# Reordering work around the matrix engine: block order, result order, half exponentials and one chunk's attention

**Chip, cores, metric.** One Trainium2 chip, one core. The time is the device time of one execution in microseconds, as a median of several executions. TensorE is called PE, VectorE DVE, ScalarE ACT, GpSimd POOL, as in the profile.

## The reference, cut to what matters

```python
# q, k, v: (8 batches, 8 heads, 576 positions, 64). Heads 0-3: local mask, heads 4-7: strided mask.
scores = np.where(masks, q @ k.T / 8, -1e9)
attn   = exp(scores - max); attn /= attn.sum()
x = (attn @ v) as (4608 tokens, 512)
h = x @ w_in                                   # 512 -> 2048        "layer 1"
g = np.maximum(h, 0) + alpha * np.minimum(h, 0)
out = g @ w_out                                # 2048 -> 512        "layer 2"
```

## The kernel before

The 4608 tokens are nine chunks of 512, numbered from 0. While PE works through the two layers of chunk n, pieces of the attention of a later batch are put between its matmuls: a score group S (into `sp` and two buffers `sph`), an attention product (PV, into `pv`), a transpose (`xp`). The kernel fixes the order on each engine. PSUM, which takes what PE computes, holds three banks for layers (`hb`), two for `sp`, and three small buffers (tag `ps`) that `sph`, `pv`, `xp` take in turn. From chunk 2 on, layer 2 works with sums and differences of blocks of g (`gsum`) and of the weights (`wsum`), so that seven products of half size do for eight.

```python
def score_both(P):                      # S: half of the scores in sp, half in two sph buffers
    ...
            if i == 0:
                nc.scalar.activation(<et from sp>, Exp); nc.gpsimd.tensor_tensor(<mask>)
                continue
            def ex(y):
                nc.scalar.activation(<half y of et from sph[y]>, Exp)
                if y: nc.gpsimd.tensor_tensor(<mask>)
            defer.extend([lambda: ex(0), lambda: ex(1)])       # one is taken per step

def pv_piece(P, a):                     # PV and its normalization
    ... nc.tensor.matmul(pv, et, v16) ...
    nc.vector.reciprocal(rc, pv[sums]); nc.vector.tensor_tensor(P.x16, pv, rc, mult)

def attn_step(end):                     # one step of attention between two pieces of a layer
    if pos["i"] < end: pieces[pos["i"]][1](); pos["i"] += 1
    while late:  late.pop(0)()          # layer-1 result gT of the block just computed
    if defer:    defer.pop(0)()

def lin1_piece(n, m):                   # layer 1, block m: 4 matmuls of 512 columns into hbank()
    ... nc.tensor.matmul(hps, win16, xT) x 4
    nc.scalar.activation(neg, hps, Relu, scale=-1)
    late.append(<nc.vector.scalar_tensor_tensor(gT[m], neg, 1-alpha, hps)>)   # frees the bank

for n in range(1, 9):
    for i in range(30):                 # (32 for n = 1)
        if i < 16: lin1_piece(n, 8 * (i % 2) + i // 2)   # for n > 1: 0, 8, 1, 9, ... 14, 7, 15
        else:
            lin2_sums(n, i - 16)        # i = 16: the DVE sums begin
            if n == 2 and i == 20: w_sums(nc.vector, (3,))
        acc += left / (19 if n == 6 else 20.5) * (0.5 if i < 16 else 1.0)
        ...                             # int(acc) attention steps follow
```

The softmax here doesn't subtract the row's maximum and nothing guards it: scores larger than these inputs give would overflow.

Of the kernel before, what the change touches and what calls it, by code (L numbers as in the profile page):

```python
# [31 lines left out]
def kernel(  # L32
# [13 lines left out]
    B, H, S, D = q.shape  # L46
# [37 lines left out]
    def hbank():  # L84

        z = next(z for z in turn if z not in busy)
        turn.remove(z)
        turn.append(z)
        return banks[z]
# [243 lines left out]
    def run_masks(P=None):  # L333

        for z in list(dmask):
            z[0] += P is None
            if z[0] > 1 or z[1] is P:
                z[2]()
                dmask.remove(z)
# [55 lines left out]
        keep(nc.gpsimd.tensor_tensor(ev, ev, m, op=ALU.mult))  # L395

    defer, defer_et = [], {}

    def score_both(P):

        w, r = P.w, 72 if P.strided else 128
        for i in range(2):
            et = ets[ectr["i"] % NE]
            ectr["i"] += 1
            if i:
                sps = [pspool.tile([128, 512], F32, tag="ps", name="sph") for _ in range(2)]
            else:
                sp = pbpool.tile([128, 2, 512], F32, tag="sp", name="sp")
                sps = [sp[:, y] for y in range(2)]
            grp = P.sgroups[i]  # L410
            n = w * len(grp)
            for x, t in enumerate(grp):
                if P.dx:
                    q0 = k0 = 80 * (4 * (2 * P.pr + t % 2) + t // 2)
                else:
                    q0, k0 = w * t, 32 + 72 * t if P.strided else 96 * t
                for y in range(2):
                    hf = slice(64 * y, 64 * y + 64)
                    keep(nc.tensor.matmul(  # L419
                        sps[y][:, w * x : w * x + w], P.kT[hf, k0 : k0 + 128],  # L420
                        P.qT[hf, q0 : q0 + w], start=(x == 0), stop=(x == len(grp) - 1),
                        skip_group_check=True))
                    P.et[(2 * (t // 2) + y, t % 2) if P.strided else (t, y)] = (et, n * y + w * x)
            ev = et[0:r, 0 : 2 * n]
            if not P.strided and i == 0:
                mv = ev.rearrange("r (y c) -> r y c", y=2)
                m = mfirst.unsqueeze(1).to_broadcast([r, 2, n])
            else:
                mv = ev.rearrange("r (c f) -> r c f", f=w)
                m = (mstr if P.strided else mother).unsqueeze(1).to_broadcast([r, 2 * n // w, w])  # L430
            if i == 0:
                keep(nc.scalar.activation(  # L432
                    ev.rearrange("r (y c) -> r y c", y=2), sp[0:r, :, 0:n], AF.Exp, scale=SCALE))
                keep(nc.gpsimd.tensor_tensor(mv, mv, m, op=ALU.mult))  # L434
                continue

            def ex(y):
                keep(nc.scalar.activation(  # L438
                    ev[:, n * y : n * y + n], sps[y][0:r, 0:n], AF.Exp, scale=SCALE))
                if y:  # L440
                    keep(nc.gpsimd.tensor_tensor(mv, mv, m, op=ALU.mult))  # L441

            defer_et["et"] = et
            defer.extend([lambda: ex(0), lambda: ex(1)])

    def pv_piece(P, a):
        run_masks(P)
        while defer and any(P.et[z][0] is defer_et["et"] for z in P.et):
            defer.pop(0)()
        if P.x16 is None:  # L450
            if P.xd and P.strided:
                P.x16 = x16s
            else:
                P.x16 = xpool.tile([128, 1024], F16, tag="x16", name="x16")
        v16 = cast16[(P.b, P.strided, "v")]
        grp = P.pgroups[a]
        r = 72 if P.strided else 128
        pv = pspool.tile([128, 512], F32, tag="ps", name="pv")
        nb = 2 * len(grp)
        for x in range(nb):  # L460
            t, hh = grp[x // 2], x % 2
            et, c = P.et[(t, hh)]
            keep(nc.tensor.matmul(  # L463
                pv[:, 65 * x : 65 * x + 65], et[0:r, c : c + 128],
                v16[0:r, 2 * P.pr + hh, t, :] if P.strided else v16[:, 6 * (2 * P.pr + hh) + t, :],
                start=(x == 0), stop=(x == nb - 1), skip_group_check=True))
        w = P.w
        rc = rpool.tile([128, 8], F32, tag="rc", name="rc")
        pvv = pv[0:w, 0 : 65 * nb].rearrange("r (c e) -> r c e", e=65)
        keep(nc.vector.reciprocal(rc[0:w, 0:nb], pvv[:, :, 64]))  # L470
        c0 = 128 * grp[0]
        keep(nc.vector.tensor_tensor(  # L472
            P.x16[0:w, c0 : c0 + 64 * nb].rearrange("r (c e) -> r c e", e=64),
            pvv[:, :, 0:64],
            rc[0:w, 0:nb].unsqueeze(2).to_broadcast([w, nb, 64]), op=ALU.mult))
# [75 lines left out]
    for g in range(7, npair + 2):  # L551
# [30 lines left out]
        for i, (kind, fn) in enumerate(seq):  # L582
            extra = []
            if todo and i in nslots:
                left = len([z for z in nslots if z >= i])
# [31 lines left out]
    def attn_until(b):  # L617

        return max(i for i, (g, _) in enumerate(pieces) if g == 4 * b + 3) + 1

    late = []

    def attn_step(end):
        run_masks()
# [11 lines left out]
    def lin1_piece(n, m):  # L636
        if m == 0:
            gTs[n] = gpool.tile([128, 16, 512], F16, tag="gT", name="gT")
        c0 = (512 * n) % RING
        parts = [(c0, 0, min(512, RING - c0))]  # L640
        if c0 + 512 > RING:
            parts.append((0, RING - c0, 512 - (RING - c0)))
        hps = hbank()
        for kk in range(4):
            for x, (src, dst, w) in enumerate(parts):
                keep(nc.tensor.matmul(  # L646
                    hps[:, dst : dst + w],
                    win16[:, kk, 128 * m : 128 * m + 128],
                    xT[:, kk, src : src + w],
                    start=(kk == 0 and x == 0),  # L650
                    stop=(kk == 3 and x == len(parts) - 1),
                    skip_group_check=True,
                ))

        neg = npool.tile([128, 512], F32, tag="neg", name="neg")
        keep(nc.scalar.activation(neg, hps, AF.Relu, scale=-1.0))  # L656

        def fin():
            keep(nc.vector.scalar_tensor_tensor(  # L659
                gTs[n][:, m, :], neg, oma[:, m : m + 1], hps, op0=ALU.mult, op1=ALU.add))  # L660
        late.append(fin)
# [31 lines left out]
    def w_sums(eng, which):  # L693

        w1, w2, w4 = wsum
        w3 = wq(0, 1)
        steps = {
            1: (w1, wq(0, 1), wq(0, 0), ALU.subtract),
            2: (w2, wq(1, 1), w1, ALU.subtract),
            3: (w3, wq(1, 1), wq(0, 1), ALU.subtract),  # L700
            4: (w4, wq(1, 0), w2, ALU.subtract),
        }
        for z in which:
            o, x, y, op = steps[z]
            keep(eng.tensor_tensor(o, x, y, op=op))

    def g_sum(eng, n, which, k0, k1):

        g = gTs[n]
        g1, g2, g4, g3 = gsum  # L710
        o, x, y, op = {
            1: (g1, quad(g, 1, 0), quad(g, 1, 1), ALU.add),
            2: (g2, g1, quad(g, 0, 0), ALU.subtract),
            3: (g3, quad(g, 0, 0), quad(g, 1, 0), ALU.subtract),
            4: (g4, quad(g, 0, 1), g2, ALU.subtract),
        }[which]
        keep(eng.tensor_tensor(o[:, k0:k1], x[:, k0:k1], y[:, k0:k1], op=op))  # L717
# [214 lines left out]
    for n in range(1, NCH):  # L932
        ab = attn_until(n + 1) if n + 1 < B else len(pieces)
        left = ab - pos["i"]
        acc = 0.0
        for i in range(32 if n == 1 else 30):
            if i < 16:
                if n > 1:
                    lin1_piece(n, 8 * (i % 2) + i // 2)
                    if i in (5, 9, 13):  # L940
                        g_sum(nc.gpsimd, n, 1, i // 2 - 2, i // 2)
                else:
                    lin1_piece(n, i)
            elif n == 1:
                lin2_piece(n, i - 16)
                if i in (18, 22, 26):
                    w_sums(nc.vector, ({18: 1, 22: 2, 26: 4}[i],))
            else:
                lin2_sums(n, i - 16)
                if n == 2 and i == 20:  # L950
                    w_sums(nc.vector, (3,))
            acc += left / (22.5 if n == 1 else 19 if n == B - 2 else 20.5) * (0.5 if i < 16 else 1.0)
            cnt = int(acc)
            acc -= cnt
            attn_n(cnt, ab)
        while pos["i"] < ab:
            attn_step(ab)
# [30 lines left out]
```

## Time and profile before

| | before |
|---|---|
| time, us (4 runs, beside the changed kernel) | 310.26 (310.14 to 310.54) |
| span of the profiled run, us | 308.5 |
| PE busy | 298.2 us, 97% |
| late starts of PE from chunk 1 on, without those around score groups | 5.39 us |

The last row is worked out from the trace: each matmul's distance to the next start, less (columns / 2400 + 0.0025) us, added up where it exceeds 0.115 us. Here and below each late start is rounded to 0.01 us before adding, as in the prediction; unrounded, the kernel before has 5.44 us. The threshold leaves out the 48 late starts of 0.09 to 0.10 us around the 24 score groups, 4.55 us in all. A PE that is "97% busy" can still start late, since the next matmul's late start hides under the modelled end of the one before. The prediction's lines show where the late starts are. They show also in one short view, the waits of PE's weight loads from 60 to 300 us (who waited for what: us in total, times, longest us; cut: two lines of score groups, L419, and one of 0.3 us at L463):

```profile
PEld L646 <- issue: 2.5, 7, 0.4
PEld L480 <- issue: 1.7, 5, 0.4
PEld L765 <- DVE gT L659: 1.6, 4, 0.4
PEld L765 <- DVE gsum L717: 1.1, 3, 0.5
```

Four kinds, 7 + 5 + 4 + 3 times: layer-1 blocks, the transpose, the first group of layer 2, the sums. "issue" means that this view found no releaser; for the first two kinds it had to be found by hand, from which buffer the matmul writes. A weight load waits a little longer than the matmul starts late (0.4 against 0.3 us), so these sums are an upper bound.

### The profile page before, as it was taken

Reading aid. Unit: us, or ns where it says so; the run is one execution under the profiler, and the core shown is the slowest. Engines: PE = TensorE matmul, PEld = TensorE weight load, DVE = VectorE, ACT = ScalarE, POOL = GpSimd, SP = SyncE. Lnnn points to the kernel's source line nnn. Section 1 sums busy time; section 2 is a strip of 40 time slices with the busy share of each in tenths; the row PEclk is TensorE's granted clock in tenths of the full one; section 3 lists DMA queues with packets and bytes.
Section 4 is the critical chain, followed back from the end, with each engine's and each line's share of the span. In section 5 each row is a group of like instructions: output and inputs, shape, how many; then the busy total and the mean of one; then the engine's idle time right before and its main releaser. Section 6 shows DMA issues by size and latency. Waiting matters only on the chain.

```text
span 308.5 us, 7042 instructions
## 1 busy us (share of the span) xinstructions
PE 298.2 (97%) x2786; PEld 190.9 (62%) x2786; DVE 223.1 (72%) x417; ACT 178.2 (58%) x330; POOL 170.9 (55%) x176
## 2 busy tenths in 40 slices
PE   8799999999999999999999999999999999999995
PEld 3464455644544478646888887458745784685484
DVE  5686857668675888488748874887579958955872
ACT  3646654697547763776467755766476336515630
POOL 8772389655999865876496629671724302101200
PEclk9999999999999999999999999999999999999999
DMA  7999999999799984999499939971911050012004
GB/s 225 195 206 207 209 214 227 178 178 283 106 163 209 170 100 48 200 237 108 71 213 212 91 54 172 139 89 30 189 53 22 0 129 31 2 58 81 0 0 138
DMA packets 81201, 40.38 MB, mean 131 GB/s; under 512 B 58624, under 2 KB 76304, under 8 KB 81168
## 3 DMA queue, kind: packets, MB, share of 16 engines
q0 software_dynamic: 41728, 17.38, 48.8%
q1 hardware_dynamic: 39168, 22.03, 32.5%
q10 hardware_dynamic: 272, 0.52, 0.6%
q8 instruction: 22, 0.36, 0.5%
q14 instruction: 11, 0.09, 0.2%
HBM read 38.01 MB, written 9.44 MB: 154 GB/s over the span
## 4 chain that ended last, share of the span: by engine, by line
PE 65%; DVE 14%; ACT 9%; DMA 4%; issue 4%; POOL 2%; SPq 0%; ACTq 0%; DVEq 0%
PE hb L646 26%; PE hb L765 20%; PE hb L673 7%; DVE gT L659 6%; DMA kl<-in_k_dram 4%; DVE x L472 3%; PE pv L463 3%; PE tp L250 2%; ACT et L432 2%; ACT neg L656 2%; ACT et L438 2%; ACT xT L502 2%; PE sp L419 1%; PE xp L480 1%; PE opl L765 1%
## 5 line engine op out<-in xcount | busy, mean ns | idle before, releaser
L646 PE MATMUL hb<-xT,win 128*128 128x512 f16 (+1 forms) x640 | 132.9, 358 | 0.7
L659 DVE SCALAR_TENSOR_TENSOR gT<-neg,oma,hb 128x512 f16<-128x512 f32 x144 | 105.1, 744 | 38.3 <-ACT neg L656 31.9
L656 ACT ACTIVATE neg<-hb 128x512 f32<-128x512 f32 x144 | 86.0, 597 | 38.6 <-PE hb L646 37.0
L646 PEld LDWEIGHTS <-win 128*128 128x128 f16 x640 | 60.0, 98 | 56.6 <-issue 2.9
L434 POOL TENSOR_TENSOR et<-et,consts 128x576 f16<-128x576 f16 (+1 forms) x24 | 30.6, 1276 | 49.4 <-ACT et L432 49.3
L717 POOL TENSOR_TENSOR gsum<-gT 128x512 f16<-128x512 f16 x21 | 24.2, 1151 | 50.6 <-DVE gT L659 50.6
L765 PEld LDWEIGHTS <-gsum 128*128 128x128 f16 x448 | 41.3, 97 | 5.9 <-DVE gsum L717 1.1
L765 PEld LDWEIGHTS <-gT 128*128 128x128 f16 x336 | 31.5, 98 | 6.6 <-DVE gT L659 1.6
L472 DVE TENSOR_TENSOR x<-pv,rc 96x384 f16<-96x384 f32 (+2 forms) x62 | 33.0, 532 | 2.1
L673 PE MATMUL hb<-wout,gT 128*128 128x512 f16 x128 | 32.4, 379 | 0.1
L441 POOL TENSOR_TENSOR et<-et,consts 128x576 f16<-128x576 f16 (+1 forms) x24 | 31.6, 1318 | 0.6 <-ACT et L438 0.6
L777 ACT COPY o<-hb 128x512 f32<-128x512 f32 (+1 forms) x28 | 15.8, 564 | 26.4 <-PE hb L765 26.4
L463 PEld LDWEIGHTS <-et 72*128 72x128 f16 (+1 forms) x448 | 23.7, 98 | 10.1 <-issue 1.3
L765 PE MATMUL hb<-wout,gT 128*128 128x256 f16 x216 | 28.0, 273 | 0.5
L765 PE MATMUL hb<-wout,gsum 128*128 128x256 f16 x216 | 26.9, 273 | 0.2 <-DVE gsum L717 0.2
L765 PE MATMUL hb<-wsum,gsum 128*128 128x256 f16 x216 | 26.3, 273 | 0.2 <-DVE gsum L717 0.2
L432 ACT ACTIVATE et<-sp 128x576 f16<-128x576 f32 (+1 forms) x24 | 15.5, 645 | 17.9 <-PE sp L419 16.2
L780 DVE TENSOR_TENSOR o<-hb,o 128x512 f32<-128x512 f32 (+1 forms) x21 | 14.2, 677 | 14.3 <-PE hb L765 10.6
L470 DVE RECIPROCAL rc<-pv 72x6 f32<-72x6 f32 (+2 forms) x80 | 14.6, 182 | 11.9 <-PE pv L463 11.6
L438 ACT ACTIVATE et<-sph 128x288 f16<-128x288 f32 (+1 forms) x48 | 18.2, 409 | 0.0
L192 POOL COPY vs<-stv 72x1024 f16<-72x1024 f16 x15 | 16.5, 1102 | 0.0
L673 PEld LDWEIGHTS <-gT 128*128 128x128 f16 x128 | 10.7, 97 | 9.1
(103 smaller groups left out, 324.4 us busy)
## 6 DMA issues: line engine op xcount, KB each, us to landing
out_dram<-o SPq DMA_DIRECT2D x27, 256.0 KB, 3.3
kl<-in_k_dram SPq DMA_DIRECT2D x6, 512.0 KB, 8.0
ql<-in_q_dram SPq DMA_DIRECT2D x5, 512.0 KB, 7.8
stv<-in_v_dram POOLq DMA_DIRECT2D x8, 288.0 KB, 7.7
vl<-in_v_dram POOLq DMA_DIRECT2D x6, 384.0 KB, 9.6
win<-in_moe_w_in_dram POOLq DMA_DIRECT2D x4, 512.0 KB, 11.8
wout<-in_moe_w_out_dram POOLq DMA_DIRECT2D x4, 512.0 KB, 13.9
out_dram<-osb SPq DMA_DIRECT2D x8, 256.0 KB, 5.4
```

The costliest lines, as they stand in the source:

```text
L432: keep(nc.scalar.activation(ev.rearrange("r (y c) -> r y c", y=2), sp[0:r, :, 0:n], AF.Exp, scale=SCALE))
L434: keep(nc.gpsimd.tensor_tensor(mv, mv, m, op=ALU.mult))
L438: keep(nc.scalar.activation(ev[:, n * y : n * y + n], sps[y][0:r, 0:n], AF.Exp, scale=SCALE))
L441: keep(nc.gpsimd.tensor_tensor(mv, mv, m, op=ALU.mult))
L463: keep(nc.tensor.matmul(pv[:, 65 * x : 65 * x + 65], et[0:r, c : c + 128], v16[0:r, 2 * P.pr + hh, t, :] if P.strided else v16[:, 6 * (2 * ...
L472: keep(nc.vector.tensor_tensor(P.x16[0:w, c0 : c0 + 64 * nb].rearrange("r (c e) -> r c e", e=64), pvv[:, :, 0:64], rc[0:w, 0:nb].unsqueeze ...
L646: keep(nc.tensor.matmul(hps[:, dst : dst + w], win16[:, kk, 128 * m : 128 * m + 128], xT[:, kk, src : src + w], start=(kk == 0 and x == 0) ...
L656: keep(nc.scalar.activation(neg, hps, AF.Relu, scale=-1.0))
L659: keep(nc.vector.scalar_tensor_tensor(gTs[n][:, m, :], neg, oma[:, m : m + 1], hps, op0=ALU.mult, op1=ALU.add))
L673: keep(nc.tensor.matmul(ops, gTs[n][:, kf, 128 * mt : 128 * mt + 128], wout16[:, kf, :], start=(kf == 0), stop=(kf == 15)))
L717: keep(eng.tensor_tensor(o[:, k0:k1], x[:, k0:k1], y[:, k0:k1], op=op))
L765: keep(nc.tensor.matmul(dst, lhs[:, kf, 128 * mt : 128 * mt + 128], rhs[:, kf, :], start=(first and own and kf == 0), stop=(kf == 7), skip ...
```

## The change

Its intent is to let PE never wait, by order alone. Four parts: (1) layer 1 ends with blocks 7, 14, 15; (2) `gT` is issued ahead of a normalization; (3) in layer 2 the first half exponential is issued at once; (4) chunk 6's attention is denser in layer 1 and pauses in the first four steps of layer 2.

```diff
     def pv_piece(P, a):
         ... matmuls into pv ...
+        while late:
+            late.pop(0)()
         nc.vector.reciprocal(...) ; nc.vector.tensor_tensor(...)
@@ score_both
-            defer.extend([lambda: ex(0), lambda: ex(1)])
+            if second["on"]:
+                ex(0)
+                defer.append(lambda: ex(1))
+            else:
+                defer.extend([lambda: ex(0), lambda: ex(1)])
@@ the loop over chunks
+            second["on"] = i >= 16
-                    lin1_piece(n, 8 * (i % 2) + i // 2)
+                    lin1_piece(n, {13: 7, 14: 14}.get(i, 8 * (i % 2) + i // 2))
-            acc += left / (22.5 if n == 1 else 19 if n == B - 2 else 20.5) * (0.5 if i < 16 else 1.0)
+            if n < B - 2 or i < 16 or i > 19:
+                acc += left / (22.5 if n == 1 else 16 if n == B - 2 else 20.5) * (0.5 if i < 16 else 1.0)
```

(`late` and `second` are declared further up; cut.)

More of the change, by code (lines that the diff above doesn't have):

```diff
@@ L397 @@
     defer, defer_et = [], {}
+    late = []
+    second = {"on": False}
     def score_both(P):
@@ L619, in attn_until @@
         return max(i for i, (g, _) in enumerate(pieces) if g == 4 * b + 3) + 1
-    late = []
     def attn_step(end):
```

## The prediction

> **What bounds the kernel now.** I read the page's shares first, then the chain of work that ended last, then the timelines of PE, DVE, ACT and POOL for chunks 2 to 7.
>
> ```profile
> span 308.5 us, 7042 instructions
> ...
> PE 298.2 (97%) x2786; PEld 190.9 (62%) x2786; DVE 223.1 (72%) x417; ACT 178.2 (58%) x330; POOL 170.9 (55%) x176
> ```
> ```profile
> 266.65 12.25 PE hb L765 x112
> 278.90 13.81 PE hb L646 x64
> ```
>
> TensorE (PE) is the bound. The two chain lines are chunk 7's layer 2 and chunk 8's layer 1, where no attention is left: 64 matmuls of 512 columns in 13.81 us are 0.2158 us each, 112 of 256 columns in 12.25 us are 0.1094 us each. These are the floor, and the change removes no matmul. So it can only win the moments in which PE starts a matmul late. I took each matmul's distance from its start to the next start in the trace, subtracted columns / 2400 + 0.0025 us, and kept what exceeds 0.08 us. From 60 us on (before that the change moves nothing) the late starts fall into two sorts. Around each score group PE loses about 0.10 us before and 0.09 us after; these belong to the small matmuls and stay. The others repeat in the same place of each chunk. Here they are in PE's timeline (start, duration, line, what; in brackets idle time and releaser):
>
> ```profile
> 104.75 3.03 PE L646 MATMUL hb<-xT,win 128*128 128x512 f16 x12
> 107.71 0.30 PE L419 MATMUL sp<-qT,kT 64*128 64x72 f16 x8
> ...
> 110.86 1.35 PE L765 MATMUL hb<-wout,gT 128*128 128x256 f16 x8
> ...
> 112.50 1.04 PE L765 MATMUL hb<-wout,gT 128*128 128x256 f16 x8
> ...
> 221.36 0.42 PE L480 MATMUL xp<-consts,x 72*128 72x72 f16 x8 [0.15 <-ACT et L438]
> ...
> 242.49 1.21 PE L765 MATMUL hb<-wsum,gsum 128*128 128x256 f16 x8 [0.20 <-DVE gsum L717]
> ...
> 244.92 1.05 PE L765 MATMUL hb<-wout,gsum 128*128 128x256 f16 x8 [0.21 <-DVE gsum L717]
> ```
>
> DVE around the same moments:
>
> ```profile
> 105.28 0.18 DVE L470 RECIPROCAL rc<-pv 96x6 f32<-96x6 f32 x1
> 105.50 0.55 DVE L472 TENSOR_TENSOR x<-pv,rc 96x384 f16<-96x384 f32 x1
> 105.97 2.08 DVE L659 SCALAR_TENSOR_TENSOR gT<-neg,oma,hb 128x512 f16<-128x512 f32 x3
> ...
> 110.67 0.55 DVE L472 TENSOR_TENSOR x16s<-pv,rc 72x384 f16<-72x384 f32 x1
> 111.14 1.39 DVE L659 SCALAR_TENSOR_TENSOR gT<-neg,oma,hb 128x512 f16<-128x512 f32 x2
> ...
> 239.40 1.35 DVE L717 TENSOR_TENSOR gsum<-gT 128x512 f16<-128x512 f16 x1
> 240.68 2.36 DVE L717 TENSOR_TENSOR gsum<-gsum,gT 128x1024 f16<-128x1024 f16 x2
> ```
>
> ACT before the late transpose, and POOL beside the slow gsum:
>
> ```profile
> 219.15 0.65 ACT L432 ACTIVATE et<-sp 128x576 f16<-128x576 f32 x1 [3.88 <-PE sp L419]
> 219.70 1.30 ACT L502 COPY xT<-xs 128x576 f16<-128x576 f16 x1
> 220.89 0.72 ACT L438 ACTIVATE et<-sph 128x288 f16<-128x288 f32 x2
> ```
> ```profile
> 239.20 1.27 POOL L434 TENSOR_TENSOR et<-et,consts 72x576 f16<-72x576 f16 x1 [2.44 <-ACT et L432]
> 240.43 1.45 POOL L441 TENSOR_TENSOR et<-et,consts 72x576 f16<-72x576 f16 x1
> ```
>
> Four kinds of lateness come out.
> **A, layer 1:** the row of 12 at 104.75 takes 3.03 us; undisturbed rows of 12 take 2.75 us. The last block waits for a hidden-layer bank (three exist), which the gT at 105.97 frees; that gT stood behind a normalization (rc and x, 0.69 us of DVE's queue). Late by 0.28, 0.28, 0.24, 0.28 us in chunks 2 to 5, 0.21 in chunk 1, 0.26 and 0.20 in chunk 6: 1.75 us.
> **B, the layer boundary:** the first eight layer-2 matmuls take 1.35 us, the next eight 1.04. The eighth needs block 7, which is computed last but one, and its gT waits behind x16s until 111.14. 0.30, 0.30, 0.28, 0.30 us in chunks 2 to 5: 1.18 us.
> **C, the transpose xp near the end of layer 2:** it needs one of three small PSUM buffers, held by the scores of the group before until ACT's first half exponential, which is queued behind a 1.30 us copy. 0.32 (chunk 1), 0.31, 0.31, 0.32, 0.31: 1.57 us.
> **D, chunk 6's layer 2:** the sums of gT come late: 0.36 + 0.15 + 0.38 = 0.89 us.
> All together 5.39 us.
>
> **What the Trainium skill says.** "Perfetto Trace Analysis", section "Optimization Strategy": a gap that repeats on the engine that should be saturated can mean too few buffers for the next tile. A and C agree, 0.28 and 0.31 us, chunk after chunk. "TensorE: Matmul & The Clock Gate", section "Wait — 56ns, not 53.3ns?": warm matmuls start N / 2.4 GHz + 2.5 ns apart, 215.7 ns at 512 columns; the trace gives 215.8. "SBUF — State Buffer", section "Who interferes with whom": a DVE instruction with two SBUF inputs contends with a GpSimd instruction that reads SBUF. The trace agrees in D: the same gsum took 0.43 us in chunk 2 with POOL free and 1.35 us at 239.40 beside the mask.
>
> **The change, part by part.** It adds and removes no operation: the instruction order of both builds has equal counts of matmuls and DVE rows. Each engine works through its queue in order, so order is all that changes.
>
> *Results ahead of normalizations (A).* Take chunk 2 with e = 0 at the start of layer 1. PE: a block 0.863 us, PV 0.19, a score group 0.46. From the old rows, a gT can start 0.71 us after its neg starts, neg starts 0.20 after the block ends, a gT takes 0.67 of DVE's queue and a normalization 0.69. Walking the new order through (PV after blocks 2, 7, 9, 14; scores after 4, 12), the gT of block 9 runs 10.50 to 11.17, and block 12 wants its bank at 11.39: no wait, where it lost 0.28. One small wait is left: block 8's gT ends at 10.50, block 11 wants to start at 10.53, with about 0.1 for the signal: 0.07 us. So chunks 2 to 5 give 1.08 - 4 x 0.07 = 0.80 us; chunk 1 its 0.21; chunk 6, with the same walk and a 0.1 rest, 0.36. Sum 1.37.
>
> *End with 7, 14, 15 (B).* Block 7 now comes before 14. Its gT is done at 15.16, the matmul wants it at 15.49 + 0.76. The 0.30 vanishes, 1.18 in all. The first part alone would do it too: without the normalization ahead, the gT of the block last but one ends 0.4 us sooner. So the two overlap and B counts once. The first sum needs blocks 14 and 15: it is finished 2.3 us after the boundary, and 3.0 is when PE reaches it.
>
> *First half exponential at once (C).* ACT then runs et, half one, copy, half two. The first half ends near 219.70 + 0.4, over a microsecond before xp wants the buffer. The copy ends 0.3 later, but its reader, the next chunk's layer 1, is over 1 us away. Saved: all 1.57. POOL's masks change places with two V copies, which nobody waits for.
>
> *Chunk 6's attention later (D).* In the new PE order the last scores come two blocks sooner, so POOL's masks are over by about boundary + 1.5 and DVE's sums start at boundary + 2.08, without the contention that doubled them; and 32 matmuls of layer 2 run on end with no normalization between the sums. But gT 15 and one normalization now stand before the first sum. It ends at 2.08 + 0.43 = 2.51, with the signal 2.57; the seventh matmul of the second product wants it at 1.75 + 0.65 = 2.40. A new wait of 0.17 us; the later sums have 0.4 us or more to spare. Saved 0.89 - 0.17 = 0.72.
>
> Sum: 1.37 + 1.18 + 1.57 + 0.72 = **4.84 us**. All of it is on the path, since PE is the path. 310.14 - 4.84 = **305.3 us** (the span 303.7).
>
> **Rivals.** *1. The waits move instead of going.* PE gets about 0.9 us less per chunk, while DVE's layer-1 queue (16 x 0.67 + 4 x 0.69 = 13.5 us of PE's 15.5) stays. Where normalizations now run later they hold PV buffers longer. For it: DVE is that full, and gT can now idle the queue while it waits for neg. Against: PE needs more than DVE, and the buffers' next users come 2 us later. If half of A and B is lost that way, 1.28 us: 306.6. *2. The later attention hurts the start of chunk 7.* Its last PV now stands one group of eight ahead of the transpose, and chunk 7's layer 1 needs that transpose and a 1.30 us copy; in the kernel before, the margin there is only about 0.1 us. It would cost up to 0.5: 305.8. *3. Transfers bind.* The DMA row shows 9s through much of the first half. But no wait for a DMA stands in the list of waits after 60 us, and the changed order starts no load markedly later. Then there would be no gain, 309 to 310; I hold it unlikely. *4. Full yield*, every rest at zero: 5.39 us, 304.75.
>
> **Range and chances.** Full yield sets a floor of 304.7; half of A and B lost plus the tail's 0.5 gives 307.1, which needs two misfortunes at once. Range 304.6 to 306.8. Over 2% faster needs 303.94, below all that I can name: 0.03. Slower: 0.01. Within 2%: 0.96.
>
> **What would show it.** PE's rows of 12 in layer 1 near 2.8 us; the first eight of layer 2 near 1.04 us in chunks 2 to 5; xp without a bracket; ACT with half an exponential before the xs copy; in chunk 6 the first gsum at 0.43 us and at most one short wait near the second product. I am wrong if PE shows new waits on gT or gsum of 0.2 us or more in chunks 2 to 5, or chunk 7's layer 1 starts with a wait on xT.

## The result

| | before | changed |
|---|---|---|
| time, us, medians of 4 runs | 310.26 | 305.37 (304.98 to 306.25) |
| ratio of fast runs | | 0.9845 (0.9822 to 0.9868) |
| span of the profiled run, us | 308.5 | 303.2 |
| late starts of PE from chunk 1 on, us | 5.39 | 0.47 |
| layer 1 of chunk 1 begins at, us | 60.91 | 60.57 |

A ratio is the mean time of one kernel's fast runs over that of the other's in the same rounds, so not quite the ratio of the medians quoted. The time fell by 4.89 us, 1.55%: within 2%, as predicted, and 0.07 us from the predicted 305.3. The span fell by 5.26 us: 4.92 us from the start of chunk 1 on, as much as the late starts fell (5.39 - 0.47), and 0.34 us came before chunk 1, where the two programs do not differ. In the traces in the fast state chunk 1 begins anywhere between 60.57 and 61.67 us, so that 0.34 is chance. Two more traces with the same single late start show it: in the changed kernel's second one chunk 1 begins 0.32 us later and the span is 0.31 us longer, in the one without the block order (below) 0.74 and 0.77 us. The sum of late starts is therefore the better measure for single parts; the times confirm it.

The profile after, first the page's head, then PE's timeline in the places that the prediction shows:

```profile
span 303.2 us, 7042 instructions
...
PE 295.4 (97%) x2786; PEld 191.6 (63%) x2786; DVE 220.7 (73%) x417; ACT 177.6 (59%) x330; POOL 169.5 (56%) x176
```
```profile
103.87 2.77 PE L652 MATMUL hb<-xT,win 128*128 128x512 f16 x12
...
109.72 1.04 PE L771 MATMUL hb<-wout,gT 128*128 128x256 f16 x8
...
118.08 0.36 PE L469 MATMUL pv<-vs,et 72*128 72x65 f16 x6 [0.30 <-DVE x16s L480]
...
217.43 0.42 PE L488 MATMUL xp<-consts,x 72*128 72x72 f16 x8
...
235.82 3.73 PE L771 MATMUL hb<-wsum,gsum 128*128 128x256 f16 x32
```

The row of 12 is down from 3.03 to 2.77 us (A), the first eight of layer 2 from 1.35 to 1.04 (B), `xp` has lost its bracket (C), and chunk 6's second and third product, 32 matmuls, run on end (D). The busy share is 97% as before: it could not tell. One new bracket has come, at 118.08. DVE and ACT at the same places:

```profile
103.96 1.39 DVE L665 SCALAR_TENSOR_TENSOR gT<-neg,oma,hb 128x512 f16<-128x512 f32 x2
105.27 0.18 DVE L478 RECIPROCAL rc<-pv 96x6 f32<-96x6 f32 x1
...
116.26 1.22 DVE L711 TENSOR_TENSOR wout<-wout 128x2048 f16<-128x2048 f16 x1
...
117.60 0.42 DVE L480 TENSOR_TENSOR x16s<-pv,rc 72x256 f16<-72x256 f32 x1
...
236.08 0.41 DVE L723 TENSOR_TENSOR gsum<-gT 128x512 f16<-128x512 f16 x1
236.41 1.28 DVE L723 TENSOR_TENSOR gsum<-gsum,gT 128x1024 f16<-128x1024 f16 x2
```
```profile
215.53 0.65 ACT L434 ACTIVATE et<-sp 128x576 f16<-128x576 f32 x1 [3.88 <-PE sp L421]
216.07 0.41 ACT L440 ACTIVATE et<-sph 128x288 f16<-128x288 f32 x1
216.36 1.31 ACT L510 COPY xT<-xs 128x576 f16<-128x576 f16 x1
```

The second gT of the pair at 103.96 is the one that PE lacked before; it now precedes the normalization. The half exponential precedes the copy. The sums of chunk 6 take 0.41 and 1.28 us instead of 1.35 and 2.36. And at 116.26 stands what the prediction missed: chunk 2's one-off weight sum, 1.22 us, in front of the normalization (rc, x16s) whose buffer the next attention product needs. In the kernel before, the same normalization ended at 118.97 us, just before that product began:

```profile
118.55 0.42 DVE L472 TENSOR_TENSOR x16s<-pv,rc 72x256 f16<-72x256 f32 x1
...
119.08 0.35 PE L463 MATMUL pv<-vs,et 72*128 72x65 f16 x6
```

### The profile page after: what moved, and what is told of

Read it like the earlier page. It is cut to its first block, busy times and chain, and to the rows that moved or that the text cites. A ratio compares the mean times of both kernels' runs of the same rounds, so it can differ in the third digit from the quotient of the medians.

```text
span 303.2 us, 7042 instructions
## 1 busy us (share of the span) xinstructions
PE 295.4 (97%) x2786; PEld 191.6 (63%) x2786; DVE 220.7 (73%) x417; ACT 177.6 (59%) x330; POOL 169.5 (56%) x176
## 4 chain that ended last, share of the span: by engine, by line
PE 88%; DVE 6%; ACT 2%; DMA 2%; issue 1%; SPq 0%; ACTq 0%
PE hb L652 41%; PE hb L771 25%; PE hb L679 8%; PE pv L469 4%; PE tp L250 2%; PE sp L421 2%; DMA kl<-in_k_dram 2%; PE opl L771 1%; DVE gsum L723 1%; DVE x L480 1%; PE xp L488 1%; DVE qT L190 1%; PE sph L421 1%; ACT kT L188 1%; PE hb L829 1%
## 5 line engine op out<-in xcount | busy, mean ns | idle before, releaser
L771 PE MATMUL hb<-wout,gT 128*128 128x256 f16 x216 | 27.3, 273 | 0.0
L440 ACT ACTIVATE et<-sph 128x288 f16<-128x288 f32 (+1 forms) x48 | 18.9, 409 | 0.0
L469 PE MATMUL pv<-vs,et 72*128 72x65 f16 x256 | 15.5, 193 | 0.7 <-DVE vs L190 0.4
```

Of the source, the lines that this page charges most:

```text
L440: keep(nc.scalar.activation(ev[:, n * y : n * y + n], sps[y][0:r, 0:n], AF.Exp, scale=SCALE))
L469: keep(nc.tensor.matmul(pv[:, 65 * x : 65 * x + 65], et[0:r, c : c + 128], v16[0:r, 2 * P.pr + hh, t, :] if P.strided else v16[:, 6 * (2 * ...
L771: keep(nc.tensor.matmul(dst, lhs[:, kf, 128 * mt : 128 * mt + 128], rhs[:, kf, :], start=(first and own and kf == 0), stop=(kf == 7), skip ...
```

## The experiments

The theory: the gain is the sum of PE's late starts, each removed by one part; parts 1 and 2 overlap at B; what PE wins in chunk 2 is partly lost at the weight sum. Rivals: one part does it all; each part acts on its own wait only; waits move rather than go. Twelve runs were made, of ten kernels, in three groups, each beside runs of the kernel before (310.35, 310.29 and 310.24 us). All but one gave the reference's result.

### Each part alone

**Results first alone**, to the kernel before:

```diff
     def pv_piece(P, a):
         ... matmuls into pv ...
+        while late:
+            late.pop(0)()
```

> The kernel before with one part alone: layer-1 results (gT) issued ahead of the normalizations. Theory 'sum of late starts': A goes (1.75 us) and B goes too (1.18 us), because the gT of block 7 no longer stands behind a normalization; in chunk 2 PE then meets the new wait of the attention product for x16s, about 0.47 us, that the changed kernel shows. C and D stay. So 1.75 + 1.18 - 0.47 = 2.5 us less, about 307.8. Rival 'each part removes its own wait': B stays in the trace (first eight layer-2 matmuls near 1.35 us), 1.3 to 1.75 us less, about 308.7. Rival 'waits move': PE's rows of 12 stay above 2.9 us somewhere else and less than 1 us is gained.

Measured: 307.86 us, ratio 0.9908 (0.9871 to 0.9944). PE's timeline at the first eight of layer 2 in chunk 2, and the waits of PE's weight loads from 60 to 300 us (the two lines of score groups cut):

```profile
111.16 1.04 PE L766 MATMUL hb<-wout,gT 128*128 128x256 f16 x8
```
```profile
PEld L483 <- issue: 1.8, 5, 0.4
PEld L766 <- DVE gsum L718: 1.1, 3, 0.5
PEld L464 <- DVE x16s L475: 0.6, 1, 0.6
```

The lines of layer-1 blocks (A) and of the first group of layer 2 (B) are gone, C and D stand, and x16s has come with 0.47 us of late start: 2.94 us in all, against 5.39. Part 2 removes B as well, so "each part its own wait" falls.

**The block order alone**, to the kernel before:

```diff
-                    lin1_piece(n, 8 * (i % 2) + i // 2)
+                    lin1_piece(n, {13: 7, 14: 14}.get(i, 8 * (i % 2) + i // 2))
```

> The kernel before with the block order 7, 14, 15 alone. Theory: B goes in chunks 2 to 5 (first eight layer-2 matmuls 1.04 us instead of 1.35), A, C and D stay; in chunk 2 the 0.3 us won there reappear as the wait for x16s, since DVE's queue there does not get shorter. 1.18 - 0.30 = 0.9 us less, about 309.3. Rival 'each part removes its own wait and nothing comes back': 1.2 us less, no wait for x16s in chunk 2.

Measured: 309.33 us, ratio 0.9972 (0.992 to 1.0024, widened by a run of 313.57). The trace is clear where the time is not: B is gone in four chunks, A, C, D stand, and the attention product of chunk 2 is 0.27 us late, which it was not before. Late starts 4.51 us, 0.88 less than before, for 0.9 expected. In its timeline:

```profile
110.78 1.04 PE L765 MATMUL hb<-wout,gT 128*128 128x256 f16 x8
```

**The half exponential alone**, to the kernel before, twice:

```diff
+            second["on"] = i >= 16
-            defer.extend([lambda: ex(0), lambda: ex(1)])
+            if second["on"]:
+                ex(0)
+                defer.append(lambda: ex(1))
+            else:
+                defer.extend([lambda: ex(0), lambda: ex(1)])
```

> The kernel before with the first half exponential issued at once in layer 2, alone. Theory: C goes in chunks 1 to 5, nothing else changes: 1.57 us less, about 308.6; xp without idle time before it. Rival: the copy of xT behind the first half ends 0.3 us later and makes the next chunk's layer 1 or a later half exponential wait, so that half or less of it, under 0.8 us, is kept.

First time: 309.58 us, ratio 0.9948 (0.9908 to 0.9989), six runs from 308.67 to 310.28; 1.0 us over the 308.6 expected. All five late starts of `xp` are gone, but the profiled run, which was the slowest, has one of 1.39 us in chunk 1, before the edit's first effect:

```profile
221.42 0.42 PE L485 MATMUL xp<-consts,x 72*128 72x72 f16 x8
```
```profile
PE sp L420 <- DMA kT<-ksd: 1.2, 1, 1.2
```

The transposing load of the keys landed 9.8 us after its issue; in the kernel before it took 7.5.

> The first half exponential at once, alone, a second time, because its first profile had a wait of 1.39 us for the transposing load of the keys at 74.5 us, ahead of any place that the edit touches. Theory: that wait is chance; without it the kernel takes 308.7, 1.57 us less than before. Rival: the edit brings it about, and it is there in this profile too, with a time near 309.6.

Second time: 308.81 us, ratio 0.9947 (0.9932 to 0.9962), the fast runs from 308.58 to 309.01. The profile fell into the slow state (clock 0.756), so no trace compares. Other traces settle it: seven fast ones, the changed kernel's two and the five of kernels made from it (below), contain this edit, and in none does PE wait for that load, which lands there 6.9 to 7.4 us after its issue. So the edit does not bring the wait about; without it C is worth 1.43 us by time of the 1.57 expected. What delayed the load that once is open.

**Chunk 6's attention alone**, to the kernel before:

```diff
-            acc += left / (22.5 if n == 1 else 19 if n == B - 2 else 20.5) * (0.5 if i < 16 else 1.0)
+            if n < B - 2 or i < 16 or i > 19:
+                acc += left / (22.5 if n == 1 else 16 if n == B - 2 else 20.5) * (0.5 if i < 16 else 1.0)
```

> The kernel before with chunk 6's attention later, alone. Theory: D goes, the three waits on gsum in chunk 6 (0.36, 0.15, 0.38 us), A's two waits in chunk 6 stay near 0.4 us in sum: 0.9 us less, about 309.3; the first gsum there takes 0.4 us instead of 1.35 because POOL's masks are over. Rival: with the normalization still ahead of the last gT the first sums come late again and a wait of 0.2 us or more stays at the second product; 0.5 us less or nothing.

Measured: 309.48 us, ratio 0.996 (0.9923 to 0.9998). Late starts 4.52 us: the three of D are gone, those of A in chunk 6 stay with 0.25 and 0.20. DVE's timeline has the first sum at its short length:

```profile
240.38 0.43 DVE L717 TENSOR_TENSOR gsum<-gT 128x512 f16<-128x512 f16 x1
```

### Why chunk 6's sums were slow

Denser attention moves two things at once: POOL's masks away from the sums, and a normalization from between them. This edit to the kernel before leaves the order as it is and only drops the last pair's masks; its result is wrong (relative error 0.21).

```diff
+                if P.g < 31:
                     nc.gpsimd.tensor_tensor(mv, mv, m, op=ALU.mult)      # mask of the first half
-                if y:
+                if y and P.g < 31:                                       # mask of the second
```

> The kernel before without POOL's two masks of the last score pair, those that run beside chunk 6's sums; a wrong result on purpose. Theory 'D is contention of POOL and DVE': the first gsum of chunk 6 takes 0.43 instead of 1.35 us, the next two 1.29 instead of 2.36, and the waits on gsum (0.89 us) go: 0.9 us faster, 309.3. Rival 'D is the normalization between the sums': the sums still come late for the third sum, 0.3 us or more of wait stays, and the gsum durations stay.

Measured: 309.41 us, ratio 0.9968 (0.9955 to 0.998). Late starts 4.53 us: D is gone entirely, with the normalization still between the sums.

```profile
239.56 0.42 DVE L718 TENSOR_TENSOR gsum<-gT 128x512 f16<-128x512 f16 x1
239.90 1.29 DVE L718 TENSOR_TENSOR gsum<-gsum,gT 128x1024 f16<-128x1024 f16 x2
```

So D was the contention of DVE's sums with POOL's masks. "SBUF — State Buffer", section "Who interferes with whom", says that a DVE instruction with two SBUF inputs contends with a GpSimd instruction that reads SBUF; here that was 0.93 us on the first sum (1.35 against 0.42) and 1.07 on the next two (2.36 against 1.29).

### Parts taken back out of the changed kernel

```diff
-                    lin1_piece(n, {13: 7, 14: 14}.get(i, 8 * (i % 2) + i // 2))
+                    lin1_piece(n, 8 * (i % 2) + i // 2)
```

> The changed kernel with the block order put back (14, 7, 15). Theory: the order is redundant once results go ahead of normalizations: block 7's gT ends about 0.1 us before its matmul wants it, so the time is that of the changed kernel, 305.4, within 0.2 us, with no wait at the layer boundary of chunks 2 to 5; chunks 7 and 8, which have no attention, may show some hundredths each. Rival 'the order is what removes B': 1.2 us slower, 306.6.

Without the block order: 305.3 us, ratio 0.9837 (0.9822 to 0.9852). Late starts 0.47 us, the same single one as in the changed kernel. Part 1 adds nothing once part 2 is there.

```diff
     def pv_piece(P, a):
         ... matmuls into pv ...
-        while late:
-            late.pop(0)()
```

> The changed kernel with the normalizations ahead of the layer-1 results again. Theory: A comes back, 1.75 us (chunk 6 perhaps 0.4 instead of 0.46), B stays away because of the order, and the x16s wait of chunk 2 shrinks from 0.47 to about 0.3: 1.5 us slower, 306.9. Rival 'waits move': no difference over 0.5 us.

With normalizations first again: 306.78 us, ratio 0.9881 (0.9866 to 0.9895). Late starts 2.00 us: A's seven, 1.74 in sum, and 0.26 at the attention product of chunk 2; B stays away. The row of 12 is back at its old length:

```profile
104.69 3.03 PE L650 MATMUL hb<-xT,win 128*128 128x512 f16 x12
```

### The wrong way round

Block 7 last of all, in the changed kernel:

```diff
-                    lin1_piece(n, {13: 7, 14: 14}.get(i, 8 * (i % 2) + i // 2))
+                    lin1_piece(n, {13: 14, 14: 15, 15: 7}.get(i, 8 * (i % 2) + i // 2))
```

This makes B large where it was avoided, and asks whether its size is understood.

> The changed kernel with block 7 computed last of all (14, 15, 7), the wrong way round on purpose. Theory: the eighth matmul of layer 2 waits for block 7's gT, which in chunks 2 to 5 stands behind a normalization: about 1.2 us in each of four chunks, 0.7 in chunk 6, 0.9 each in chunks 7 and 8, less the 0.47 us of chunk 2 that is hidden then: 6.8 us slower, 312.2. Rival: the order of the blocks has no weight once results go first, 305.4; or only the plain chain of about 0.9 us shows in each chunk, 311.

Measured: 311.89 us, ratio to before 1.005 (1.0036 to 1.0064), so 6.45 us slower than the changed kernel on the same chip (305.44). Late starts: 1.17, 1.17, 1.16, 1.17 in chunks 2 to 5, 0.68 in chunk 6, 0.87 and 0.87 in chunks 7 and 8, and no wait for x16s; 7.09 us in all.

```profile
110.02 0.93 PE L771 MATMUL hb<-wout,gT 128*128 128x256 f16 x7
111.95 0.28 PE L771 MATMUL hb<-wout,gT 128*128 128x256 f16 x1 [1.00 <-DVE gT L665]
```

Seven matmuls start on time, the eighth waits for block 7. With the order as in the change the same wait is none. So the order of blocks has weight when it is wrong, but between 7 last but one and 7 last but two there is no difference once results go first.

### The wait that was left

The weight sum of chunk 2 has its user only at the fifth product (i = 24).

```diff
-                if n == 2 and i == 20:
+                if n == 2 and i == 22:
                     w_sums(nc.vector, (3,))
```

> The changed kernel with the one-off weight sum of chunk 2 (1.22 us of DVE) issued two layer-2 steps later, behind the normalization that PE waits for. Theory: the one wait left after 60 us, 0.47 us at the attention product of chunk 2, is DVE's queue and goes: 0.4 to 0.5 us faster, 304.9, PE's late starts after 60 us then those around score groups alone. Rival: the wait is not the weight sum's (DVE is behind by itself) and moves to a later product or the sum is then late for its own user at the fifth product: no difference.

First look: 304.9 us, ratio 0.9837 (0.9809 to 0.9865), one of six runs at 307.75. No late start is left from chunk 1 on but those around score groups. DVE now runs the normalization first:

```profile
116.81 0.42 DVE L480 TENSOR_TENSOR x16s<-pv,rc 72x256 f16<-72x256 f32 x1
117.15 1.21 DVE L711 TENSOR_TENSOR wout<-wout 128x2048 f16<-128x2048 f16 x1
```

Then side by side with the changed kernel:

> The changed kernel itself, beside the three others of this call on one chip. 305.3; one wait of 0.47 us after 60 us, at chunk 2's attention product. Where a run is a microsecond longer, the transposing load of chunk 1's keys landed late, not the changed order.

> The changed kernel with chunk 2's weight sum two steps later, on the same chip as the changed kernel: 0.4 to 0.5 us faster than it if the wait for x16s is the weight sum's; no difference if the first look at it was luck of the loads at the start.

Measured: the changed kernel 305.44 us, ratio 0.9845 (0.9829 to 0.9861); with the sum later 304.88 us, 0.9828 (0.9812 to 0.9843). The medians differ by 0.56 us for 0.47 in the traces; the intervals of the ratios overlap, so by time alone it is not proved, but both traces of each kernel agree (0.47 and 0.47 against none and none). What was expected of runs a microsecond longer, that the key load is late in them, stays untested: none of these was profiled. The kernel with the sum later is the best kernel: 1.7% below the kernel before.

## Why the prediction was right

- **The bound and the 5.39 us.** Right. With all parts and the later weight sum, no late start is left but those around score groups; PE's rows run at the floor that the prediction took from chunks without attention.
- **A, 1.37 us of 1.75.** The mechanism is right (taking part 2 back out brings 1.74 us back). The size was too small: all seven late starts went. The rests of 0.07 a chunk and 0.1 in chunk 6 came as 0.02 at most, below the threshold. The walk itself was close: in chunk 2 of the change's trace block 8's gT ends 10.49 us after the start of layer 1, against 10.50. What it had too large was the signal: the matmul that needs the bank starts 0.054 us after that gT's end, not 0.1.
- **B, 1.18 us.** Right, and so is the overlap: part 1 alone or part 2 alone removes it, and together they count once.
- **C, 1.57 us.** Right in the trace; 1.43 us by time.
- **D, 0.72 of 0.89 us.** Contention as the cause is right. The new wait came where it was expected but smaller, 0.07 us and not 0.17, below the threshold: the first sum began 2.01 us after the boundary, not 2.08, and ended at 2.42; the seventh matmul of the second product, due at 2.40, started at 2.47.
- **What was missed.** The prediction looked for new waits on gT, gsum and xT, and checked chunk 2's buffers only up to the layer boundary. It left out the weight sum, which chunk 2 alone has. In the kernel before, the attention product there had no slack: x16s ended at 118.97 us and the product began at 119.08. Counted from the start of the chunk, PE came 0.58 us sooner (A and B) and DVE's weight sum only 0.08, and 0.47 us turned into the new wait.
- **The sum, 4.84 us.** The trace has 4.92, the time 4.89. That it is this close is luck: two errors nearly cancel, rests of 0.55 us of which about 0.15 came, and a wait of 0.47 us that was not foreseen.
- **Rivals.** "Waits move" was true in one place, by 0.47 us. The tail of chunk 7 lost nothing. Transfers do bind now and then: the key load of chunk 1 cost one profiled run 1.39 us, but not through the change.

## What to carry to other kernels

When an engine is 97% busy, add up how late each instruction starts against its own floor, and sort the late starts by place; that sum is the most that removing these waits can give. Here it was 5.39 us: the change won 4.92, the later weight sum the other 0.47. The 4.55 us around score groups are as large in the changed kernel; no run tried an order with fewer of them. Removing a wait brings the engine sooner to the next one: check slack at every later place, above all where one repetition differs from the rest. Try each part alone and each part left out: here one of four parts was redundant, which the result of the whole could not show.

## What the Trainium skill lacked or had wrong

- "TensorE: Matmul & The Clock Gate", section "Back-to-back issue gap", gives about 131 ns for each matmul of 512 columns in a stream of weight loads and matmuls, and calls the 216 ns of its formula an over-count. Here 64 such pairs on end take 13.81 us, 215.8 ns each: the formula holds for the stream.
- No page has a figure for passing between matmuls of 128 and of 64 rows; "TensorEngine Tiling (Array Packing)", section "Key Properties", names a drain at a change of tiling mode, without its size. In all fast traces PE loses about 0.10 us before and 0.09 us after each score group, whose matmuls have 64 rows; that the row count is the cause is not tested.
- "SBUF — State Buffer", section "Who interferes with whom", has the contention right but no measured durations for two element-wise operations of this kind: a sum of 0.42 us took 1.35 beside POOL's mask, and the next mask 1.45 instead of 1.27.
- No page accounts for the slow execution met once: 383.06 us instead of 308.8, with a span of 381.3 us at a mean clock of 0.756 in its profile, from a program on one core. "TensorE: Matmul & The Clock Gate", section "Seeing it yourself", says of the limit at 13/16 of the clock that one or two busy cores never trip it; 0.756 is below 13/16, and what else ran on the chip the runs do not tell.
